# The three written orders of issue of a slot attention and feed-forward kernel, replaced

## The chip, the cores and the metric

The kernel runs on one core of a Trainium2 chip. The time is device microseconds (us) of one launch on that core; lower is better. The median of three runs stands for a kernel, and one further execution is recorded by the hardware profiler. The engines are TensorE (PE: matmuls, with weight loads as PEld), VectorE (DVE), ScalarE (ACT), GpSimd (POOL) and SyncE (SP), which here issues the DMA transfers. Each engine works off its own instructions in program order and waits, at its next instruction, for what that one needs.

## The reference

Attention between 512 positions and 32 slots in both directions, for 8 batches of 8 heads of 64; the reads are joined to 544 rows of 512 per batch. Then a LayerNorm with a gain, a feed-forward layer of 2048 with ReLU, and the residual:

```python
scores = scale * np.matmul(x, state.transpose(0, 1, 3, 2))      # x (8, 8, 512, 64), state (8, 8, 32, 64)
xread = np.matmul(softmax(scores), state)
scores2 = scale * np.matmul(state, x.transpose(0, 1, 3, 2))
sread = np.matmul(softmax(scores2), x)
y = concat([xread, sread], axis=2)                               # to (8, 544, 512)
xn = (y - mu) / np.sqrt(var + 1e-06) * g_ln
out = y + np.maximum(xn @ w_ch1, 0.0) @ w_ch2                    # w_ch1 (512, 2048), w_ch2 (2048, 512)
```

## The kernel before, in words

Every operand of a feed-forward matmul is carried as two 16-bit parts, a high one and a remainder, and a product is the sum of three terms (`TERMS`): high by high and the two mixed ones. The high part is written by ACT and the remainder by DVE.

The 2048 hidden columns are cut into four units u of 512. In each the first product (`first_product`, line 549) is done by seven block products m0 to m6 of twelve matmuls each (line 565). They are of a fast 2 by 2 matrix multiplication: its operands are seven sums of blocks of the normalised rows (the pieces `pc`, which the DMA transposes to `xnT`) and seven of the weight (`w1c`). Their results are put together from the accumulators in `strips`: ACT copies, DVE adds (u2, u3 and their second halves), POOL adds once. ReLU (ACT) and its remainder (DVE) give `hid`. A strip is named here by its unit and what it is: u0 m4 is the fifth product of unit 0. The second product (`second_product`, line 601) multiplies `hid` by `w2h`, twelve matmuls for each unit and each of four row blocks c (line 605), with a DVE add per row block (`xr`) and a store per pair of them.

`attention(b)` (line 251) is one stream of 121 items: loads of x and state (SP), their scale (an absolute maximum, brought across partitions by two small matmuls into `spread`), the 16-bit parts `x` (the program's x16) and `sh`, the transfers that transpose them (`sT`, `xT`, two of the latter), score0 and score1 (line 299), both softmaxes, the transposed weights `ebT`, the read (line 341), the fold (line 354), the exchange of `ea` through DMA (`ek`), the mix into `xr`, and `normalise` (line 406): statistics, the rows `xn`, the pieces, and four transposes to `xnT`. These are called xnT0, xnT2, xnT4 and xnT6 after the first piece in each.

The order of all this is written out by hand. Each function is a generator that yields one item (an instruction or a group of them) after the other, and `issue` takes from several such streams in the order of a string: `a3` is item 3 of the first stream, `b4-6` are items 4 to 6 of the second. Within a stage the order in the string is the program order of every engine's row:

```python
with tc.manual_schedule():
    for item in plan.split() or [...]:
        n = [int(k) for k in item[1:].split("-")]
        drain(streams[ord(item[0]) - ord("a")][n[0]:n[-1] + 1])
```

There are three strings.
- `PLAN` (line 37) is the first stage. Its streams: a is the attention of batch 0, b to e prepare the four units of the first weight (`weights1`, line 482; `raw` in, `w1c` out), f is the first products of batch 0, g to j prepare the second weight (`weights2`, line 516; `w2h`), k is the attention of batch 1, l is the second products of batch 0.
- `BATCH` (line 60) is used six times, for b = 1 to 6: a is the first products of batch b, b its second products, c the attention of batch b + 1.
- `LAST` (line 70): a and b are the products of batch 7, c normalises the 256 state rows of all batches (`state_rows`, line 642, loaded back into `xs`), d and e are their products, half as wide.

Between stages the rows are joined by the tile scheduler: the loads of the next batch stand ahead of some of the last transfers of this one.

Of the kernel before, what the change touches and what calls it, by code (L numbers as in the profile page):

```python
# [34 lines left out]


PLAN = (
# [22 lines left out]
BATCH = (  # L60
# [9 lines left out]
LAST = (  # L70
# [10 lines left out]


class Later:
# [605 lines left out]
```

## Time and profile before

| what | value |
|---|---|
| median of three runs | 857.88 us (855.61 to 859.16) |
| the profiled execution's own time | 858.59 us |
| its span in the trace | 856.5 us |
| mean granted TensorE clock | 0.983 |
| PLAN | 0 to 204.1 us |
| six times BATCH | 204.1 to 730.7 us |
| LAST | 730.7 to 856.5 us |

The first three rows are one launch seen in three ways: the span is what the trace covers, from the first instruction to the last. The stages' bounds are the starts of the first product matmul of the next stage on PE. In rows of the timeline a line holds start, length, engine, source line, operation, what it writes and reads by the program's names, how many instructions were joined, and in brackets the idle time ahead of it with what ended that. Nearly all ACT, DVE, POOL and SP work is recorded by the helper `do` and so has its line, 105; it is told apart by the names of what it writes. In this section's table and in the prediction a batch means a run of BATCH, counted from 1.

### The profile page before, as it was taken

How to read it: one execution, taken by the hardware profiler on the slowest of the kernel's cores; microseconds unless marked ns; L12 is line 12 of the kernel's file. 1: busy time of each engine (PE TensorE's matmuls, PEld its weight loads, DVE VectorE, ACT ScalarE, POOL GpSimd, SP SyncE). 2: the span in 40 equal slices, each digit the busy share in tenths (PEclk: the TensorE clock that was granted, in tenths of full speed). 3: DMA queues.
4: the chain of work that ended last, by engine and by line, in shares of the span. 5: the costliest groups of instructions: out<-in, count | busy, mean ns of one | idle time of the engine just before them, and what ended most of it. 6: DMA issues, size and time to landing. Idle time of an engine off the chain costs nothing.

```text
span 856.5 us, 13363 instructions
## 1 busy us (share of the span) xinstructions
PE 727.6 (85%) x5472; PEld 481.8 (56%) x5472; DVE 550.1 (64%) x894; ACT 373.9 (44%) x624; POOL 143.2 (17%) x101
## 2 busy tenths in 40 slices
PE   0130786699799979998999989998999899999997
PEld 0030554556674667557754865486548654775663
DVE  5899886896784477557755675567556756573330
ACT  4685763554453345136523652365236523342220
POOL 1606001210130112111202120212020202120100
PEclk9999988799999999999999999999999999999999
DMA  9961522336324521362236222623262423302000
GB/s 278 297 180 57 141 98 51 96 96 136 56 46 98 135 57 26 102 131 51 51 79 131 69 56 60 152 56 66 55 149 54 76 53 76 85 2 44 26 25 25
DMA packets 152861, 75.45 MB, mean 88 GB/s; under 512 B 131744, under 2 KB 143520, under 8 KB 152352
## 3 DMA queue, kind: packets, MB, share of 16 engines
q1 hardware_dynamic: 152656, 74.34, 36.1%
q8 instruction: 43, 0.70, 0.4%
q10 hardware_dynamic: 144, 0.26, 0.1%
q14 instruction: 18, 0.15, 0.1%
HBM read 28.57 MB, written 9.44 MB: 44 GB/s over the span
## 4 chain that ended last, share of the span: by engine, by line
PE 69%; DVE 13%; DMA 9%; ACT 3%; issue 3%; SPq 1%; POOL 1%; POOLq 0%; DVEq 0%; ACTq 0%
PE acc L605 38%; PE acc L565 27%; DMA xT<-x 4%; DVE strips L105 2%; DVE w1c L105 2%; DVE hid L105 2%; DVE x L105 2%; ACT raw L105 2%; DVE w_t L105 1%; SPq L105 1%; PE banks L341 1%; PE banks L354 1%; DMA x_f<-in_x_dram 1%; DMA ek<-ek 1%; POOL strips L105 1%
## 5 line engine op out<-in xcount | busy, mean ns | idle before, releaser
L565 PE MATMUL acc<-xnT,w1c 128*128 128x256 f16 (+1 forms) x3024 | 333.1, 270 | 35.5 <-DMA xnT<-pc 23.4
L605 PE MATMUL acc<-w2h,hid 128*128 128x512 f16 x1632 | 360.7, 379 | 0.0
L565 PEld LDWEIGHTS <-w1c 128*128 128x128 f16 x3024 | 284.5, 99 | 85.5 <-issue 43.3
L605 PEld LDWEIGHTS <-hid 128*128 128x128 f16 x1632 | 158.1, 98 | 180.7
L105 ACT ACTIVATE hid<-strips 128x512 f16<-128x512 f32 (+1 forms) x144 | 85.2, 604 | 100.8 <-DVE strips L105 59.4
L105 DVE SCALAR_TENSOR_TENSOR hid<-strips,hid 128x512 f16<-128x512 f32 (+1 forms) x144 | 108.0, 767 | 28.6 <-ACT hid L105 27.8
L105 ACT ACTIVATE strips<-acc,hs 128x512 f32<-128x512 f32 (+1 forms) x96 | 61.7, 659 | 125.9 <-PE acc L565 119.3
L105 DVE SCALAR_TENSOR_TENSOR strips<-acc,hs,strips 128x512 f32<-128x512 f32 (+1 forms) x96 | 68.1, 711 | 67.0 <-PE acc L565 63.8
L105 POOL TENSOR_TENSOR strips<-strips 128x512 f32<-128x512 f32 (+1 forms) x36 | 47.0, 1304 | 381.9 <-DVE strips L105 299.0
L105 DVE BATCH_NORM_STATS2 s<-xr 128x6 f32<-128x512 f32 x32 | 20.7, 685 | 48.5 <-ACT xr L105 48.5
L105 DVE SCALAR_TENSOR_TENSOR xr<-acc,uo,xr 128x512 f32<-128x512 f32 x28 | 20.9, 749 | 34.6 <-PE acc L605 34.6
L105 ACT ACTIVATE xr<-banks,ux 128x1024 f32<-128x1024 f32 x14 | 15.6, 1115 | 60.5 <-PE banks L381 60.5
L105 ACT ACTIVATE pc<-tq 128x512 f16<-128x512 f32 (+1 forms) x27 | 16.3, 605 | 49.1 <-DMA xnT<-pc 33.1
L105 PE MATMUL spread<-idf,w_am 128*2 128x128 f32 x8 | 2.7, 337 | 39.9 <-ACT raw L105 39.9
L105 DVE TENSOR_TENSOR pc<-xn,pc 128x512 f16<-128x512 f32 (+1 forms) x36 | 24.9, 714 | 14.5 <-ACT pc L105 14.5
L105 ACT ACTIVATE xn<-xn,rs 128x512 f32<-128x512 f32 x34 | 22.1, 712 | 25.9 <-POOL rs L105 25.1
L105 POOL TENSOR_TENSOR rs<-rs,mhalf 128x4 f32<-128x4 f32 (+1 forms) x9 | 12.3, 1371 | 126.2 <-DVE rs L105 122.9
L105 DVE TENSOR_TENSOR pc<-tq,pc 128x512 f16<-128x512 f32 (+1 forms) x27 | 24.1, 892 | 10.9 <-ACT pc L105 10.9
L105 DVE SCALAR_TENSOR_TENSOR x<-x_f,x_s,x 128x512 f16<-128x512 f32 x32 | 30.1, 959 | 0.2 <-ACT x L105 0.2
L299 PE MATMUL banks<-xT,sT 128*32 128x512 f16 x128 | 11.1, 435 | 22.4 <-DMA xT<-x 14.9
L105 ACT ACTIVATE pc<-xn 128x512 f16<-128x512 f32 (+1 forms) x36 | 19.9, 597 | 21.0 <-DMA xnT<-pc 21.0
L105 POOL TENSOR_TENSOR ts<-ts,mA 128x1024 f32<-128x1024 f32 x8 | 15.3, 1913 | 68.8 <-DVE mA L105 68.8
(115 smaller groups left out, 631.9 us busy)
## 6 DMA issues: line engine op xcount, KB each, us to landing
raw<-in_moe_w_ch_dram SPq DMA_DIRECT2D x16, 1024.0 KB, 5.8
x_f<-in_x_dram SPq DMA_DIRECT2D x16, 512.0 KB, 5.3
out_dram<-xr SPq DMA_DIRECT2D x16, 512.0 KB, 3.5
ek<-ea SPq DMA_DIRECT2D x56, 64.0 KB, 2.0
ek<-ek SPq DMA_DIRECT2D x7, 512.0 KB, 4.1
s_r<-in_state_dram SPq DMA_DIRECT2D x32, 64.0 KB, 4.5
xnT<-pc SPq DMA_TRANSPOSE x36, 4.3
s_j<-in_state_dram SPq DMA_DIRECT2D x8, 64.0 KB, 5.1
```

The source lines that it names most:

```text
L105: return lambda: f(*map(now, args), **{k: now(v) for k, v in kw.items()})
L299: nc.tensor.matmul(ps[32 * j:32 * j + 32, g], lhsT=sT[:, g, a, 32 * j:32 * j + 32], rhs=xT[:, 4 * g + j].rearrange("p c t -> p (c t)"), st ...
L341: nc.tensor.matmul(ps_z[:, h // 4, :, h % 4], lhsT=x16[:, h * C + c].rearrange("p i d -> p (i d)"), rhs=ebT[:, :, h // 4, c, 32 * (h % 4): ...
L354: nc.tensor.matmul(pr[:, g], lhsT=z4[:, g, i], rhs=fold, start=i == 0, stop=i == 1, skip_group_check=True)
L565: nc.tensor.matmul(ps[:, f * w:(f + 1) * w], lhsT=w1u[:, m, i, k, f * P:(f + 1) * P], rhs=xTk[:, m, j, k], start=begin and f == 0 and k == ...
L605: nc.tensor.matmul(po, lhsT=hid[:, i, q, c * P:(c + 1) * P], rhs=w[:, j, q], start=first and q == 0 and n == 0, stop=last and q == 3 and n ...
```

## The change

Only the three strings differ. Each new string holds the same items as the one it replaces (592, 235 and 258 of them), in another order; streams, loops, tiles and instructions are the same. The new strings take three lines fewer, so line 105 of before is line 102 afterwards, 299 is 296, 565 is 562 and 605 is 602. A line or two of each:

```diff
 PLAN = (
-    "a3 a2 b1 c1 a1 a0 b0 a4-5 c0 a6-13 a27 a60 a17 a28 b6 a18 b7 a22 b8 a24 a14 a25 b9 b20 a23 a19 d1 c7 c6 "
...
+    "c1 a3-4 a0-2 a5-12 c0 b0 a13 a19-20 c7 a14-15 c6 a27 c8 b1 a24-25 a22 a17 c2 a23 c3-4 a18 c9 a28 a60 c5 "
...
 BATCH = (
-    "a23 c0-2 a0 a24 c5 c4 c6 c3 a27 a1 c8 a6 c7 a28 a25 c11 c10 a36 c9 a26 a7 c12-13 a37 a42 a8 c14 a38 a9 "
...
+    "a25 a23-24 a0-1 c1 c9-10 c0 c7 a2 a26 a33 a3 a34 c2 c11 c8 c12 a4-5 a10 c13-14 a6-7 a11 c15 a12 a27 "
...
 LAST = (
-    "a25 c1 c0 a23 a27 a24 c4 a42 a28 a26 c2 a36 c5 c3 c10 a33 a37 a73 c8 a38 a34 a29 a39 a35 a71 a30 c6 a31 "
...
+    "a4-5 c0 c2-3 a23-26 c1 c4-6 c8 a0 c10 a33-34 a2 c7 c9 c15-16 a13 a1 a3 c11-13 a14-15 a6-8 a10-12 a29 a16 "
...
```

In stream a of BATCH items 0 to 22 are unit 0, 23 to 45 unit 1 and so on, so a25 is u1 m1 and a10 is u0 m4. PE's row in a batch began u1 m0, u0 m0 and had 16 products ahead of score1, one between it and score0; now it begins u1 m1, u1 m0, u0 m0, u0 m1, u1 m4 and has 18 products ahead of both, which follow each other. In PLAN the attention of batch 0 and of batch 1 (streams a and k) and the products (f) stand earlier against the weights (b to e, g to j), and the pieces of the normalised rows come in the order 1, 0, 2, 3 instead of 2, 0, 3, 1.

**SP's row, from the transposes at the end of one batch to the softmax of the next, before.** `xnT` are the transposed pieces, `xT` and `sT` the transposed x16 and state, `s_r` a quarter of the state rows, `x_f` and `s_j` the loads of x and state for the batch after.

```order
L105 DMA_TRANSPOSE xnT<-pc 128x16x128 x2
L105 DMA out_dram<-xr 128x1024
L105 DMA_TRANSPOSE xnT<-pc 128x8x128
L105 DMA_TRANSPOSE xnT<-pc 128x16x128
L105 DMA out_dram<-xr 128x1024
L105 DMA_TRANSPOSE xT<-x_3432 128x16x128
L105 DMA_TRANSPOSE sT<-sh 128x4x128
L105 DMA_TRANSPOSE xT<-x_3432 128x16x128
L105 DMA_TRANSPOSE ebT<-eb 128x16x128
```

Now:

```order
L102 DMA_TRANSPOSE xnT<-pc 128x16x128 x2
L102 DMA_TRANSPOSE xnT<-pc 128x8x128
L102 DMA_TRANSPOSE xnT<-pc 128x16x128
L102 DMA out_dram<-xr 128x1024
L102 DMA sread_rows<-sread 64x1x64
L102 DMA out_dram<-xr 128x1024
L102 DMA_TRANSPOSE sT<-sh 128x4x128
L102 DMA s_r<-in_state_dram 32x8x64 x3
L102 DMA_TRANSPOSE xT<-x_3424 128x16x128 x2
L102 DMA s_r<-in_state_dram 32x8x64
L102 DMA_TRANSPOSE ebT<-eb 128x16x128
```

The three loads of `s_r` moved from the end of the batch before to between `sT` and the two `xT`, which now follow each other, and a fourth behind them; `sT` came ahead of both `xT`.

**DVE's row at the end of a batch, before.** `tq` and `pc` are the sums and remainders of the pieces, `xr<-acc` is the add of a row block of the second product.

```order
L105 SCALAR_TENSOR_TENSOR xr<-acc,uo,xr 128x512 x2
L105 TENSOR_TENSOR tq<-xn 128x512
L105 TENSOR_TENSOR pc<-xn,pc 128x512
L105 TENSOR_TENSOR tq<-xn,tq 128x512
L105 TENSOR_TENSOR pc<-tq,pc 128x512
L105 TENSOR_TENSOR pc<-xn,pc 128x512
L105 TENSOR_TENSOR pc<-tq,pc 128x512
L105 SCALAR_TENSOR_TENSOR xr<-acc,uo,xr 128x512
L105 TENSOR_TENSOR pc<-tq,pc 128x512
L105 TENSOR_TENSOR pc<-xn,pc 128x512 x2
L105 SCALAR_TENSOR_TENSOR xr<-acc,uo,xr 128x512
```

Now, the same place (`hid` here are the remainders of unit 3's strips m5, r and u2):

```order
L102 TENSOR_TENSOR tq<-xn 128x512
L102 TENSOR_TENSOR tq<-xn,tq 128x512
L102 TENSOR_TENSOR pc<-xn,pc 128x512
L102 TENSOR_TENSOR pc<-tq,pc 128x512 x2
L102 TENSOR_TENSOR pc<-xn,pc 128x512
L102 SCALAR_TENSOR_TENSOR hid<-strips,hid 128x2x256 x2
L102 TENSOR_TENSOR pc<-tq,pc 128x512
L102 SCALAR_TENSOR_TENSOR hid<-strips,hid 128x2x256
L102 TENSOR_TENSOR pc<-xn,pc 128x512 x2
L102 SCALAR_TENSOR_TENSOR xr<-acc,uo,xr 128x512 x4
```

The adds of the row blocks moved behind all pieces, and the last three remainders of the first product came between the pieces.

**DVE's row where LAST begins, before.** `xs` are the state rows, `strips` ahead of or between their statistics is the add u1 u2 that u1 m4 waits for.

```order
L105 SCALAR_TENSOR_TENSOR xr<-acc,uo,xr 128x512
L105 BN_STATS s_6922<-xs 128x6
L105 SCALAR_TENSOR_TENSOR strips<-acc,hs,strips 128x512
L105 BN_STATS s_6939<-xs 128x6
L105 BN_AGGR mv<-s_6922 128x2
L105 BN_AGGR mv<-s_6939 128x2
```

Now:

```order
L102 SCALAR_TENSOR_TENSOR xr<-acc,uo,xr 128x512 x4
L102 BN_STATS s_6895<-xs 128x6
L102 BN_AGGR mv<-s_6895 128x2
L102 SCALAR_TENSOR_TENSOR strips<-acc,hs,strips 128x512
L102 BN_STATS s_6929<-xs 128x6
L102 BN_AGGR mv<-s_6929 128x2
```

The aggregate of the first pair moved ahead of the add to `strips`; the first statistics stand ahead of it in both.

73 rows, old and new, of tables (BATCH, LAST, PLAN) are left out of this document.

## The prediction

> **What bounds the kernel now.** I read the page first: the span, the busy shares, the 40 slices and the chain that ended last.
>
> ```profile
> span 856.5 us, 13363 instructions
> PE 727.6 (85%) x5472; PEld 481.8 (56%) x5472; DVE 550.1 (64%) x894; ACT 373.9 (44%) x624; POOL 143.2 (17%) x101
> PE   0130786699799979998999989998999899999997
> DVE  5899886896784477557755675567556756573330
> PE 69%; DVE 13%; DMA 9%; ACT 3%; issue 3%; SPq 1%; POOL 1%; POOLq 0%; DVEq 0%; ACTq 0%
> ```
>
> TensorE (PE) bounds everything behind the first five slices; ahead of them VectorE (DVE) is the full one. The same instructions run afterwards, so PE still needs its 727.6 us, and only the 129 us in which it does nothing can change. The windows put that idle time into stages (start:end, length, busy time of PE, PEld, DVE, ACT, POOL, clock, DMA share, GB/s):
>
> ```profile
> 0.00:91.80 91.80, 14.57 (x167) 11.19 (x168) 75.64 (x129) 56.89 (x86) 32.68 (x27) 1.00 0.67 197
> 91.80:204.10 112.30, 94.56 (x631) 61.33 (x631) 93.08 (x158) 59.67 (x95) 14.02 (x9) 0.89 0.40 101
> 204.10:292.50 88.40, 83.39 (x622) 54.97 (x621) 55.67 (x87) 37.54 (x63) 14.07 (x9) 1.00 0.40 83
> 292.50:382.40 89.90, 84.64 (x620) 55.38 (x618) 54.53 (x87) 37.43 (x63) 14.09 (x9) 0.98 0.37 79
> 382.40:469.30 86.90, 83.12 (x621) 54.84 (x620) 55.67 (x87) 37.55 (x63) 14.08 (x9) 1.00 0.38 83
> 642.80:730.70 87.90, 83.19 (x621) 54.81 (x620) 55.47 (x86) 37.55 (x63) 14.08 (x9) 1.00 0.31 66
> 730.70:856.50 125.80, 118.08 (x961) 79.73 (x959) 48.80 (x87) 32.17 (x65) 11.99 (x11) 0.99 0.12 33
> ```
>
> PLAN runs to 204.1, the six runs of BATCH to 730.7, LAST to the end. PE is idle 77.2 us until the first product, 17.7 in the rest of PLAN, 3.7 to 5.3 in each BATCH (the two that are not shown are like the third), 7.7 in LAST.
>
> **BATCH, the largest term (six times).** PE's timeline, from the start of the batch at 382.41, names its waits, and that of DVE and SyncE (SP) the work behind the last of them:
>
> ```profile
> 382.41 8.02 PE L565 MATMUL acc<-xnT,w1c 128*128 128x256 f16 x72
> 400.23 5.40 PE L565 MATMUL acc<-xnT,w1c 128*128 128x256 f16 x48 [1.41 <-DVE strips L105]
> 406.78 0.62 PE L299 MATMUL banks<-xT,sT 128*32 128x512 f16 x8 [1.14 <-DMA sT<-sh]
> 410.03 0.62 PE L299 MATMUL banks<-xT,sT 128*32 128x512 f16 x8 [1.23 <-DMA xT<-x]
> 401.02 0.75 DVE L105 SCALAR_TENSOR_TENSOR x<-x_f,x_s,x 128x512 f16<-128x512 f32 x1
> 401.85 1.33 SPq L105 DMA_TRANSPOSE xT<-x  x1
> 403.28 1.94 SPq L105 DMA_TRANSPOSE sT<-sh  x1
> 405.61 1.85 SPq L105 DMA_TRANSPOSE xT<-x  x1
> xT<-x SPq DMA_TRANSPOSE x2, 4.4
> ```
>
> Three waits, 1.41 + 1.14 + 1.23 = 3.78 us: a product (u0 m4) behind DVE's add; score1 behind sT's landing; score0 behind the second xT (issued 405.61, 4.4 us to landing).
> - The first goes: on DVE the add that u0 m4 needs is now second in the batch, no longer behind seventeen others.
> - SP now issues sT and three s_r loads ahead of both xT. xT1 still waits for the last x16 remainder, at about +19.2 of the batch (now 401.85 - 382.41 = 19.44), but xT0 no longer waits behind sT: about +21.1 (now +23.2). It lands at +25.5 to +26.0.
> - PE now has 18 products ahead of both scores. A product of 12 matmuls takes 8.02 / 6 = 1.34 us, its rows overlapping (1.31 apart); 18 of them and the small matmuls bring PE to score0 at about +24.5. So one wait of 1 to 1.5 us takes the place of three: 3.78 - 1.5 = 2.3, and I count **2.2 us a batch**, 13.2 in six.
> - Batches 1, 2 and 6 take 88.4, 89.9 and 87.9 where the third takes 86.9: 5.5 us together. In batch 2 it is a longer wait for the same xT with slower products behind it:
>
> ```profile
> 321.44 0.82 PE L299 MATMUL banks<-xT,sT 128*32 128x512 f16 x8 [2.72 <-DMA xT<-x]
> 322.19 10.76 PE L565 MATMUL acc<-xnT,w1c 128*128 128x256 f16 x84
> ```
>
> 84 products' matmuls at 8.02 / 72 each would be 9.36, so the 2.72 us wait cost 1.4 more behind it. An earlier xT takes some of this excess away; between 0 and 5.5 I take 2.3. BATCH together: **-15.5**, bounds -20 (every wait gone but 0.5) and -4 (below, where its margins give way).
>
> What costs nothing here: the four s_r loads moved on SP (1.9 us of issue) stand where SP waits for the remainders anyway; if xT were ready sooner, they would cost up to that. ACT's and POOL's rows move with DVE's (37.5 and 14.1 us busy of 87); where one of ACT's evictions falls behind `ea` the margin is about 0.6 us. The softmax items move to where their inputs arrive, under products.
>
> The price is at the batch's end. DVE there does the eight LayerNorm pieces in one block, with two remainders of the last unit (u3) behind four of them, another behind pc6's, and all four output adds last:
>
> ```profile
> 455.81 1.76 DVE L105 TENSOR_TENSOR tq<-xn,tq 128x512 f32<-128x512 f32 x1
> 457.49 0.68 DVE L105 TENSOR_TENSOR pc<-tq,pc 128x512 f16<-128x512 f32 x1
> 464.07 0.69 DVE L105 TENSOR_TENSOR pc<-tq,pc 128x512 f16<-128x512 f32 x1 [1.61 <-ACT pc L105]
> 467.96 1.29 DVE L105 TENSOR_TENSOR pc<-xn,pc 128x512 f16<-128x512 f32 x2 [3.19 <-ACT pc L105]
> 458.85 4.98 SPq L105 DMA_TRANSPOSE xnT<-pc  x2
> 455.43 1.59 POOL L105 TENSOR_TENSOR xn<-xn 128x512 f32<-128x512 f32 x1 [4.34 <-DVE tq L105]
> ```
>
> Summing such durations from the end of mix to u3's remainders gives about 18.9 us, and PE comes to the second product that reads them after 19.2 to 19.4: 0.1 to 0.5 us to spare. A DVE operation beside one of POOL's takes 1.76 instead of 0.68, so one collision more turns that into a wait of 1 us. I take it as kept.
>
> **PLAN.** The first product waits for xnT, and that chain is DVE's own row:
>
> ```profile
> 91.84 5.34 PE L565 MATMUL acc<-xnT,w1c 128*128 128x256 f16 x27 [23.41 <-DMA xnT<-pc]
> 87.30 12.66 SPq L105 DMA_TRANSPOSE xnT<-pc  x4
> 84.32 2.35 DVE L105 TENSOR_TENSOR pc<-xn,pc 128x512 f16<-128x512 f32 x2
> L105 DVE SCALAR_TENSOR_TENSOR w1c<-w_t,w_s,w1c 128x512 f16<-128x512 f32 x11 | 10.7, 1006 | 0.0
> L105 DVE TENSOR_SCALAR raw<-raw 128x1024 uint32<-128x1024 uint32 x12 | 8.6, 721 | 0.0
> 137.08 1.04 PE L299 MATMUL banks<-xT,sT 128*32 128x512 f16 x8 [6.45 <-DMA xT<-x]
> 158.53 1.87 PE L341 MATMUL banks<-ebT,x 128*128 128x64 f16 x32 [6.54 <-DMA ebT<-eb]
> ```
>
> Ahead of the remainder that releases xnT0, DVE has two w1c remainders (1.01 each), three shifts of raw (0.72), two other pieces (half of 2.35 and one of 0.68 above, 1.9) and sread fewer: 2.0 + 2.2 + 1.9 + about 1.5 of small ones = 7.6. So xnT0 would be issued near 79.7 instead of 87.30, and the first product would start near 84.2. That is no gain yet. The weight work moved behind it is still due, PE waits for it (the w2 scale's broadcast near 93, u2's weights near 100) and then, at score0 of the second batch's attention, now early in PE's row, for xT near 116. Past that, attention(1) stands far earlier on DVE: the remainder of eb after 121 us of DVE work, not 135, so the 6.54 us wait for ebT goes, and the 6.45 us wait for xT turns into the one near 116. By hand I find PE about 4 us ahead at 138 and PLAN's end at 195 to 197.5, so **-6.5**. Bounds: 0, when all is handed back at the waits named, and -12, when the first product's lead is kept (7.6) with most of the ebT wait.
>
> **LAST.**
>
> ```profile
> 739.28 18.50 PE L565 MATMUL acc<-xnT,w1c 128*128 128x256 f16 x168 [1.87 <-DVE strips L105]
> 737.88 0.70 DVE L105 BATCH_NORM_STATS2 s<-xs 128x6 f32<-128x512 f32 x1 [6.23 <-DMA xs<-sread_rows]
> 739.74 0.30 DVE L105 BATCH_NORM_AGGREGATE mv<-s 128x2 f32<-128x6 f32 x2
> 758.87 3.33 PE L565 MATMUL acc<-xnT,w1c 128*128 128x256 f16 x29 [1.08 <-ACT strips L105]
> ```
>
> DVE's row still begins with the state rows' statistics, which wait for a load, ahead of the add that u1 m4 needs. PE now reaches u1 m4 one product earlier and the add has the aggregate ahead of it too: 1.87 + 1.31 + about 0.2 = 3.4 us, 1.5 more; the 1.08 us wait may go. Bounds -1 and +1.5, I take **+0.5**. The tail (one add, four stores) is the same instructions in the same order.
>
> **Sum.** 858.59 (the profiled execution; its span is 856.5, and it lies 0.7 above the median of 857.88) - 15.5 - 6.5 + 0.5 = **837.1**.
>
> **Rivals.**
> - *PLAN gives nothing.* The earlier first product is handed back at score0's wait near 116 and later at w2's weights. For it: DVE is 83% busy in PLAN's second part. Against: 13 us in two waits for attention(1) stand there now. 858.6 - 15.5 + 0.5 = 843.6.
> - *BATCH's margins give way.* A second product waits 1 to 2 us for u3's remainders in each batch: 6 x 1.5 = 9 back, and PLAN as forecast: 846.
> - *More of both* (PLAN -10, BATCH -18): 831.
> - *The clock pays.* The single wait for xT0 becomes 2.7 us, as at 321.44, and each batch then pays 1.2 more in the wait and 1.4 behind it: 6 x 2.6 = 15.6, so 852.7. Against: waits of 1.1 to 1.4 us in the third batch cost no clock (1.00). The Trainium skill's page "TensorE: Matmul & The Clock Gate", section "Part 1: The HAM clock gate (the "warmup" mystery)", has the clock halved only after an idle window of about 3.4 us; by that, no wait foreseen in BATCH would cost clock and this rival is void. The row with 10.76 does not agree: there 2.72 us was enough.
> - *Slower than before.* DVE stops in its row at the remainder of pc6, which waits for ACT's pc6 and this for xnT2's landing; behind it stand a remainder of u3, two more pieces and all four output adds. Now pc6 starts 464.07 - 458.85 = 5.2 us after the first xnT issue, and I find 2.5 us to spare. It decides past 7.7 us; each us beyond costs six. To eat the 21.5 gained and 4.3 more it takes 25.8 / 6 = 4.3 us beyond, a landing 12 after the issue, and gives 863. Against: the row at 467.96, behind the pair's second transfer, came 9.1 after the first issue, and no transfer here was slower.
>
> **How the numbers follow.** Chances: forecast (831 to 844) 0.44; PLAN nothing 0.17; margins 0.17; more of both 0.08; clock 0.07; slower 0.07. What a measurement of this kernel tells from no change is about 0.5%, 4.3 us, so faster means under 854. Faster: 0.44 + 0.17 + 0.08, 0.14 of the margins' case (it may take two places in a batch) and 0.02 of the clock's = 0.85; same: 0.03 + 0.05 = 0.08; slower 0.07. The range takes in -20 and -12 in part, 826, and the clock's case, 853; outside are the slower case and some 0.1 of the tails.
>
> **What would show it.** Right: the first product near 84; BATCH windows of 84 to 85 us with one wait ahead of score0 and none at u0 m4 or score1; PLAN ending at 195 to 198; u1 m4 in LAST waiting 3 us or more. Wrong: a wait of PE for `hid` or `xr` late in the batches (margins), products past 0.12 us a matmul behind score0 (clock), PLAN's end near 204, or a DVE idle stretch ahead of pc6 with the adds behind it.

## The result, and the profile after

The changed kernel takes 826.97 us (median of 4 runs, 825.11 to 827.74), before it was 857.95 (4 runs, the three above and one more): the ratio is 0.9639, with a 95% interval of 0.9613 to 0.9665. The profiled execution took 826.83 us, its span is 825.0. The page of the profile after, its first lines and the chain that ended last:

```profile
span 825.0 us, 13446 instructions
PE 725.5 (88%) x5472; PEld 481.6 (58%) x5472; DVE 540.8 (66%) x894; ACT 366.2 (44%) x624; POOL 151.4 (18%) x101
PE   0140868899999999998999999999999999899997
DVE  4999879795767476746774676567656765662221
PE 73%; DVE 14%; DMA 7%; issue 3%; ACT 3%; SPq 0%; DVEq 0%; ACTq 0%
```

PE's busy time is the same within 2.1 us (727.6 before); the idle time went from 129 to 99.5 us. By stages (windows of the changed kernel, columns as before):

```profile
0.00:83.20 83.20, 15.32 (x167) 11.54 (x168) 70.85 (x120) 52.68 (x80) 35.89 (x27) 1.00 0.72 207
83.20:193.40 110.20, 94.55 (x631) 59.91 (x631) 94.27 (x166) 63.00 (x101) 15.87 (x10) 0.92 0.47 115
193.40:277.70 84.30, 82.74 (x620) 54.99 (x619) 54.73 (x87) 36.49 (x63) 14.59 (x9) 1.00 0.40 85
362.10:446.90 84.80, 82.58 (x620) 54.91 (x619) 54.76 (x87) 36.50 (x63) 14.57 (x9) 1.00 0.41 92
446.90:530.60 83.70, 82.69 (x621) 54.98 (x620) 54.76 (x87) 36.48 (x63) 14.57 (x9) 1.00 0.38 85
698.20:825.00 126.80, 119.33 (x961) 80.41 (x959) 47.28 (x87) 31.54 (x65) 12.21 (x11) 0.99 0.10 29
```

From these bounds, read off the first product matmul of each stage:

| stage | before | after | difference | forecast |
|---|---|---|---|---|
| to the first product | 91.84 | 83.23 | -8.6 | -7.6 |
| all of PLAN | 204.15 | 193.41 | -10.7 | -6.5 |
| six times BATCH | 526.55 | 504.80 | -21.75 | -15.5 |
| LAST, to PE's end | 121.04 | 122.05 | +1.0 | +0.5 |
| behind PE's end | 4.8 | 4.7 | 0 | 0 |

The fourth batch shows what the prediction spoke of. PE's timeline from its start, and SP's:

```profile
446.95 9.33 PE L562 MATMUL acc<-xnT,w1c 128*128 128x256 f16 x84
457.95 13.27 PE L562 MATMUL acc<-xnT,w1c 128*128 128x256 f16 x120
471.15 0.61 PE L296 MATMUL banks<-xT,sT 128*32 128x512 f16 x8
472.78 0.61 PE L296 MATMUL banks<-xT,sT 128*32 128x512 f16 x8 [1.01 <-DMA xT<-x]
460.19 1.22 SPq L102 DMA_TRANSPOSE sT<-sh  x1
461.46 1.56 SPq L102 DMA_DIRECT2D s_r<-in_state_dram  x3
465.87 4.46 SPq L102 DMA_TRANSPOSE xT<-x  x2
```

One wait of 1.01 us, ahead of score0, where three of together 3.7 us stood; the 18 products and score1 run without a break up to it. (In the second batch score1 waits too: 0.72 us, and then score0 1.00.) xT is issued at 465.87 - 446.95 = +18.9 of the batch. At the batch's end DVE and PE stand as close as foreseen:

```profile
518.72 1.28 DVE L102 SCALAR_TENSOR_TENSOR hid<-strips,hid 128x512 f16<-128x512 f32 x2
521.74 0.69 DVE L102 TENSOR_TENSOR pc<-tq,pc 128x512 f16<-128x512 f32 x1 [1.74 <-ACT pc L102]
519.79 10.96 PE L602 MATMUL acc<-w2h,hid 128*128 128x512 f16 x50
```

The two remainders of u3 (strips m5 and r) are done at 520.00; the second product that reads r's begins at 520.22 in the middle of PE's unbroken run, which ends at 530.58 with four products of 2.59 us. That is 0.2 us to spare, counted to the start of the product. In the program its third matmul is the first that reads a remainder (the third of `TERMS`), and in run 7 the wait stands there (46 of the four products' 48 matmuls come behind it), so the margin was up to 0.4 us wider.

### The profile page after: what moved, and what is told of

It is laid out like the page before. It is cut to its first block, busy times and chain, and to the rows that moved or that the text cites. A ratio compares the mean times of both kernels' runs of the same rounds, so it can differ in the third digit from the quotient of the medians.

```text
span 825.0 us, 13446 instructions
## 1 busy us (share of the span) xinstructions
PE 725.5 (88%) x5472; PEld 481.6 (58%) x5472; DVE 540.8 (66%) x894; ACT 366.2 (44%) x624; POOL 151.4 (18%) x101
## 4 chain that ended last, share of the span: by engine, by line
PE 73%; DVE 14%; DMA 7%; issue 3%; ACT 3%; SPq 0%; DVEq 0%; ACTq 0%
PE acc L602 41%; PE acc L562 28%; DMA xT<-x 4%; DVE x L102 2%; DVE w1c L102 2%; DVE strips L102 2%; DVE w_t L102 1%; DMA x_f<-in_x_dram 1%; DVE hid L102 1%; PE banks L378 1%; PE banks L338 1%; DVE raw L102 1%; ACT raw L102 1%; PE banks L351 1%; PE banks L296 1%
## 5 line engine op out<-in xcount | busy, mean ns | idle before, releaser
L102 ACT ACTIVATE hid<-strips 128x512 f16<-128x512 f32 (+1 forms) x144 | 80.5, 597 | 78.5 <-DVE strips L102 43.3
L102 DVE SCALAR_TENSOR_TENSOR hid<-strips,hid 128x512 f16<-128x512 f32 (+1 forms) x144 | 92.1, 663 | 16.4 <-ACT hid L102 16.2
L102 DVE TENSOR_TENSOR pc<-xn,pc 128x512 f16<-128x512 f32 (+1 forms) x36 | 35.9, 1013 | 10.8 <-ACT pc L102 10.7
L102 POOL TENSOR_TENSOR ts<-ts,mA 128x1024 f32<-128x1024 f32 x8 | 17.2, 2149 | 92.7 <-DVE mA L102 90.0
L102 DVE SCALAR_TENSOR_TENSOR strips<-acc,hn,strips 128x512 f32<-128x512 f32 (+1 forms) x32 | 22.8, 711 | 16.1 <-PE acc L562 15.2
L102 ACT ACTIVATE pc<-xn 128x512 f16<-128x512 f32 (+1 forms) x36 | 20.8, 595 | 17.9 <-DMA xnT<-pc 17.8
L102 DVE TENSOR_TENSOR pc<-tq,pc 128x512 f16<-128x512 f32 (+1 forms) x27 | 18.2, 691 | 11.6 <-ACT pc L102 11.6
L102 ACT ACTIVATE ea<-ef 128x1024 f16<-128x1024 f32 x8 | 8.4, 1055 | 38.0 <-DVE ef L102 38.0
```

Of the source, the lines that this page charges most:

```text
L102: return lambda: f(*map(now, args), **{k: now(v) for k, v in kw.items()})
```

## The experiments

Ratios are to the kernel before, run on the same chip. The changed kernel itself stands at 0.9639.

**1 to 3: each string alone.** Before's program with one of the three new strings.

```diff
-PLAN = (before)      BATCH = (before)      LAST = (before)
+PLAN = (after)       # e1, the others as before
+BATCH = (after)      # e2
+LAST = (after)       # e3
```

> Before with the new PLAN alone. If the three stages add up, the whole of PLAN's share of the difference shows: the first batch's first product at 193.4 instead of 204.2, so -10.7 us (847). If PLAN's lead is used up later (the first batch waits for loads or transposes that are not earlier), between 0 and -5. The forecast had -6.5 for this stage.

> Before with the new BATCH alone. If the stages add up: six batches in 504.8 instead of 526.6 us, -21.8 us (836). If part of the gain belongs to the state that PLAN leaves behind, less: the forecast's own terms give -13 to -15.5 (843).

> Before with the new LAST alone: u1 m4's wait grows from 1.87 to 2.7 us and more, +1.0 us (859) if the stages add up. A rival, that this loss comes only from the new batch's late last add ahead of the load of xs, would give -0.5 to 0.

Measured: PLAN alone 846.1 us, ratio 0.9870 (0.9852 to 0.9888); BATCH alone 835.28, 0.9746 (0.9730 to 0.9761); LAST alone 859.26, 1.0015 (0.9999 to 1.0031). As parts of 858 us that is -11.2, -21.8 and +1.3, together -31.7, and the whole change measured -31. In the traces PLAN ends at 193.56 in the first, the six batches take 505.5 in the second, and LAST 122.9 in the third. The stages add up. In the third the added time alone is within its measurement's uncertainty; its trace shows it (122.9 against 121.0), with a wait of 3.35 us ahead of u1 m4.

**4: the first of the three waits of a batch, alone.** In the kernel before one add moves ahead on DVE.

```diff
-... a2 a5 c32 c34 c30 a40 c35 c26 c33 a19 a3 c24 ...
+... a2 a5 c32 c34 a3 c30 a40 c35 c26 c33 a19 c24 ...
```

> Before with one item of BATCH moved: the add that u0 m4 waits for (u0 u2) stands ahead of two x16 remainders on DVE. Its wait of 1.42 us goes in both theories. If the three waits of a batch are worth their sum, -1.42 x 6 = -8.5 us. If they are one chain that ends at the second xT's landing, PE reaches score1 and score0 earlier, waits there 1.4 us longer, and the time does not move (0 to -1).

Measured: 857.8 us, ratio 1.0016 (0.9998 to 1.0033). PE's timeline of the third batch:

```profile
393.36 6.84 PE L564 MATMUL acc<-xnT,w1c 128*128 128x256 f16 x61
408.00 1.01 PE L298 MATMUL banks<-xT,sT 128*32 128x512 f16 x8 [2.67 <-DMA sT<-sh]
408.94 2.71 PE L564 MATMUL acc<-xnT,w1c 128*128 128x256 f16 x12
411.59 0.61 PE L298 MATMUL banks<-xT,sT 128*32 128x512 f16 x8
```

The wait ahead of u0 m4 is gone and score1's has grown from 1.14 to 2.67. The three waits were one chain, and what ends them is the landing of sT and xT. Of the 2.2 us a batch that the prediction summed, none comes from the add alone. (Behind the longer wait twelve matmuls take 2.71 us, not 1.47; more on that below.)

**5: sT between the two xT again.** The changed kernel, one item moved on SP.

```diff
-... c22 c23 a13 a14 ... c33 c20 a47 c37 ...
+... c22 a13 a14 ... c33 c23 c20 a47 c37 ...
```

> The changed kernel with one item of BATCH moved on SP alone: sT stands between the two xT again. The second xT is then issued 1.7 us later and lands near +27.0 of the batch, so the one wait ahead of score0 grows from 1.0 to about 2.2 us: +1.2 x 6 = +7 us. If a wait of that length also costs clock (the rival of the forecast), 1.4 more in each batch: +15. If the position of sT does not matter, 0.

Measured: 840.23 us, ratio 0.9791 (0.9769 to 0.9813), 13.3 above the changed kernel. PE's timeline of the third, fourth and fifth batch:

```profile
393.12 0.61 PE L296 MATMUL banks<-xT,sT 128*32 128x512 f16 x8 [3.86 <-DMA xT<-x]
393.67 5.77 PE L562 MATMUL acc<-xnT,w1c 128*128 128x256 f16 x36
...
479.78 1.04 PE L296 MATMUL banks<-xT,sT 128*32 128x512 f16 x8 [2.37 <-DMA xT<-x]
480.76 5.23 PE L562 MATMUL acc<-xnT,w1c 128*128 128x256 f16 x36
...
566.28 0.61 PE L296 MATMUL banks<-xT,sT 128*32 128x512 f16 x8 [2.33 <-DMA xT<-x]
566.83 4.10 PE L562 MATMUL acc<-xnT,w1c 128*128 128x256 f16 x36
```

The waits ahead of the scores add up to 16.0 us in the six batches against 8.5 in the changed kernel: +7.5, as the first theory has it. The batches together take 12.6 longer (517.4 against 504.8), and the 5 us that are left are products at a lower clock in three of them (granted 0.98 in the first, third and fourth, 1.00 in the others): behind the waits of 3.86 and 2.37 us the same 36 matmuls took 5.77 and 5.23 us, behind 2.33 they took 4.10. So both theories were half right: a wait of such a length may cost some 1.6 us more, or nothing.

**6: more products ahead of the scores.** The changed kernel with u3 m1 (a71) ahead of them.

```diff
-... a47 c37 c76 a37 c28 a49 a51 c36 ... c49 a71 a52 ...
+... a47 a71 c37 c76 a37 c28 a49 a51 c36 ... c49 a52 ...
```

> The changed kernel with one more product (u3 m1) ahead of the two scores. If that wait is only a matter of how many products stand ahead, 1.0 us a batch goes, -6 to -7 us in all. If the softmax chain behind it has no room left (ebT's landing has 1.6 us ahead of the read, the exchange of ea 0.9 ahead of mix), part of it comes back as waits there: -2 to -4. If there is no room at all, 0.

Measured: 828.58 us, ratio 0.9647 (0.9630 to 0.9665): no gain. PE's timeline at the second and fifth batch:

```profile
320.58 1.09 PE L338 MATMUL banks<-ebT,x 128*128 128x64 f16 x32 [1.18 <-DMA ebT<-eb]
...
586.04 0.79 PE L378 MATMUL banks<-sk,ek 128*128 128x64 f16 x16 [1.55 <-DVE strips L102]
```

The waits ahead of score0 are gone in four batches and smaller in two (0.42 and 1.07); new ones stand ahead of the read (0.61, 1.18) and of mix (0.44, 1.55, 1.37). In the fifth batch of the changed kernel the last exchange of `ek` is issued at 580.54 and lands 4.1 us later, at about 584.65, and mix starts at 584.75: score0 to mix is a chain about as long as PE's work beside it. In this run that exchange is issued at 581.50 and takes up to 4.5 us; the wait of 1.55 ends with it, though the row names `strips`, which DVE had finished at 585.36. A later start comes back as a wait further on: the six batches take 504.8 us in both.

**7: one remainder behind pc6.** The changed kernel; b3, the second product that reads it, follows it in the string.

```diff
-... a87 c112 a78 b3 c118 c119 a85 ...
+... a87 c112 c118 c119 a78 b3 a85 ...
```

> The changed kernel with one remainder of unit 3 (r) on DVE moved two places, behind the remainder of pc6, which waits for xnT2's landing. If DVE's order at the batch's end is the tight place that the forecast named (0.2 us to spare now), the second product that reads it waits until about 523.1 where it starts at 520.2 in the fourth batch: 2.9 x 6 = +17 us, and a wait of that length in each batch may cost clock besides (+25). If DVE has room there, 0.

Measured: 849.36 us, ratio 0.9885 (0.9858 to 0.9912), 22.4 above the changed kernel. DVE's and PE's timeline in the fourth batch of this run:

```profile
534.69 0.69 DVE L102 TENSOR_TENSOR pc<-tq,pc 128x512 f16<-128x512 f32 x1 [2.34 <-ACT pc L102]
535.30 1.28 DVE L102 SCALAR_TENSOR_TENSOR hid<-strips,hid 128x512 f16<-128x512 f32 x2
536.04 4.28 PE L602 MATMUL acc<-w2h,hid 128*128 128x512 f16 x19 [2.27 <-DVE hid L102]
```

DVE stands still for 2.34 us at pc6 and PE with it; five batches show such a wait (2.24 to 2.33), the sixth one of 0.58, and PE's busy time rises by 6.9 us, to 732.4, through slower matmuls. This is the margins' rival, and the slower case in small: two places in DVE's row cost 19.6 us in the six batches (524.4 against 504.8); PLAN, 2.1 longer, is within its scatter, and LAST took 1.7 more.

**8 and 9: LAST's first wait.** In 8 only the add (a26) goes ahead of the first statistics; in 9 the state rows' first eleven items go behind the first products' copies and adds.

```diff
-a4-5 c0 c2-3 a23-26 c1 c4-6 c8 a0 c10 a33-34 a2 c7 c9 c15-16 a13 a1 a3 c11 ...
+a4-5 c0 a23-26 c2-3 c1 c4-6 c8 a0 c10 a33-34 a2 c7 c9 c15-16 a13 a1 a3 c11 ...      # e8
+a4-5 c0 a23-26 c1 a0 a33-34 a2 a13 a1 c2-3 a3 c4-6 c8 c10 c7 c9 c15-16 c11 ...      # e9
```

> The changed kernel with one add of LAST (u1 u2) ahead of the first statistics of the state rows on DVE. The wait of 2.73 us ahead of u1 m4 goes: -2.5 to -2.9 us. If another wait stands right behind it (an accumulator that is not free, or a later strip on DVE behind the statistics that wait for xs), -0.5 to -1.5.

> The changed kernel with the first eleven items of the state rows in LAST (statistics, xn, the first pieces) moved, on DVE, ACT and POOL alike, behind the first products' own copies and the add u1 u3. The load of xs then holds up nothing that PE waits for early: 2.7 us less, 824.3. If the add u0 u2 or a later strip still stands behind the statistics, about half of it, 825.6; if the wait only moves again, as when the add alone was moved, 0.

Measured: 828.13 us (ratio 0.9648, 0.9633 to 0.9663) and 826.14 us (0.9623, 0.9599 to 0.9646). The first is a miss. Its PE and ACT timelines:

```profile
712.26 3.00 PE L562 MATMUL acc<-xnT,w1c 128*128 128x256 f16 x26 [2.63 <-ACT strips L102]
710.46 0.72 ACT L102 ACTIVATE xn<-xn,rs 128x512 f32<-128x512 f32 x1 [6.66 <-POOL rs L102]
711.54 0.67 ACT L102 ACTIVATE strips<-acc,hs 128x512 f32<-128x512 f32 x1
```

The wait moved three products on: on ACT, too, a copy that PE needs stands behind work on the state rows. With all of them moved (9), LAST takes 118.0 us to PE's end instead of 122.05, 4.05 less, with no wait left. That is more than the wait's 2.73: behind it, in the changed kernel, products also ran slowly. Its DVE row shows the load that all of this waits for:

```profile
704.73 0.69 DVE L102 BATCH_NORM_STATS2 s<-xs 128x6 f32<-128x512 f32 x1 [5.57 <-DMA xs<-sread_rows]
698.21 5.40 PE L562 MATMUL acc<-xnT,w1c 128*128 128x256 f16 x48
706.34 5.92 PE L562 MATMUL acc<-xnT,w1c 128*128 128x256 f16 x40 [2.73 <-DVE strips L102]
```

By the second row 40 matmuls take 4.5 us; they took 5.92. Over the whole kernel the two medians, taken on different chips, differ by 0.8 us, which doesn't separate 9 from the changed kernel; its trace shows the gain in LAST and longer other stages (PLAN 0.9, the third batch 1.5). The latter is clock, at the same order: the third batch of the changed kernel, and that of run 9.

```profile
389.15 0.62 PE L296 MATMUL banks<-xT,sT 128*32 128x512 f16 x8 [2.22 <-DMA xT<-x]
389.70 4.10 PE L562 MATMUL acc<-xnT,w1c 128*128 128x256 f16 x36
...
390.20 1.04 PE L296 MATMUL banks<-xT,sT 128*32 128x512 f16 x8 [2.10 <-DMA xT<-x]
391.17 5.27 PE L562 MATMUL acc<-xnT,w1c 128*128 128x256 f16 x36
```

Runs 7, 8 and 11, in which the order around the scores is the same, show it as run 9 does (waits of 2.21, 2.32 and 2.35; the 36 matmuls took 5.25, 5.09 and 5.13). The profiled execution of the changed kernel was the lucky one of five.

**10: two products fewer ahead of the scores.**

```diff
-... a36 a18 a46 a8 a48 a9 c33 c20 a47 c37 c76 a37 c28 a49 a51 c36 c39 a38 c40 c4 c34-35 c38 c49 a71 ...
+... a36 a18 a8-9 c20 c76 a37 c33 c37 c28 c36 c39-40 c4 c34-35 c38 c49 a46 a48 a47 a49 a51 a38 a71 ...
```

> The changed kernel with two products (u2 m0, u2 m1) behind the scores instead of ahead of them in PE's row of BATCH, DVE's maximum and transpose for the softmax ahead of the add that reads them. If the time of a batch is the landing of the second xT plus PE's work behind score0, the wait there grows by 2 x 1.31 and so does each batch: 1.31 x 2 x 6 = +15.7 us, and up to 1.5 a batch more where the longer wait costs clock (+25). If a batch is set by the chain from score0 to mix instead, those products fill room behind score0 and the time stays within 3 us.

Measured: 853.2 us, ratio 0.9937 (0.9914 to 0.9960), 26.2 above the changed kernel: the upper figure. The waits ahead of the scores add up to 23.5 us, 15.1 more than in the changed kernel (2 x 1.31 x 6 = 15.7 was expected); the other 11 is clock (PE's busy time is 736.0, 10.5 more). The third batch:

```profile
396.45 0.62 PE L296 MATMUL banks<-xT,sT 128*32 128x512 f16 x8 [1.79 <-DMA xT<-x]
398.82 0.61 PE L296 MATMUL banks<-xT,sT 128*32 128x512 f16 x8 [1.76 <-DMA xT<-x]
399.37 8.39 PE L562 MATMUL acc<-xnT,w1c 128*128 128x256 f16 x60
```

In this run's sixth batch, behind waits of 1.67 and 1.87 us, 60 such matmuls took 6.72 us. With the changed kernel both ways round (6 and 10), its place of the scores is a good one: one product later gains nothing, two earlier lose 26 of the 31 us; one earlier was not measured.

**11: the first product's lead given back.** In PLAN six DVE operations on weights return to where they delay xnT0, with four ACT items that feed them.

```diff
-... b19 a93 a91 d20 e22 a94 f2 f0 e30 e24-25 g2 d17 h7 d21-22 e31 e23 a95 ... h4 ... g3 ...
+... b19 e22 e30 e24-25 e31 e23 h7 h4 g2-3 a93 a91 d20 a94 f2 f0 d17 d21-22 a95 ...
```

> The changed kernel with six DVE operations on weights (three w1c remainders, two shifts, one 'or', 4.8 us by their durations) put back ahead of the pieces that release xnT0 in PLAN. The first product then starts near 88 instead of 83.2. If the lead of the first product is kept to the end of PLAN, +4.8 us (832). If it is handed back at score0's wait for xT near 106 to 113, as the forecast argued, 0 to +1 (827 to 828), and the gain of PLAN is then the earlier attention of the second batch.

Measured: 830.66 us, ratio 0.9688 (0.9662 to 0.9713), 3.7 above the changed kernel. PE's timeline:

```profile
87.25 5.69 PE L562 MATMUL acc<-xnT,w1c 128*128 128x256 f16 x36 [19.85 <-DMA xnT<-pc]
118.12 1.04 PE L296 MATMUL banks<-xT,sT 128*32 128x512 f16 x8 [6.78 <-DMA xT<-x]
```

In the changed kernel the same rows are at 83.23 [15.38] and 112.90 [6.80]. The wait ahead of score0 doesn't shrink when the first product comes later; the transfer it waits for comes later too. PLAN ends at 198.72, where the eight traces with the changed kernel's PLAN end at 192.5 to 195.5. So the lead is kept to the end of PLAN, other than the forecast argued.

**12: the x16 remainders sooner, with 9's LAST.** On DVE alone, in BATCH and PLAN. In the program either xT waits for the last of the four remainders, not for its own two: xT is taken from the pair of buffers that held x_f, which all four read.

```diff
 BATCH
-... a13 a14 c5 c26 c31-32 a19 c29-30 c27 a28 c24 a20 a35 a40 c25 ...
+... a13 c5 c26-27 a14 c31-32 a19 c29-30 a28 c24-25 a20 a35 a40 ...
 PLAN
-... k34-35 a57 f15-16 d34 g17 k29 k23 f21 k32 k28 k36 k30 k33 ...
+... k34 k32 a57 f15 d34 k29-30 k35 f16 g17 k23 f21 k28 k36 k33 ...
```

> The changed kernel with the state rows of LAST later (as in the ninth run), and on DVE alone the x16 remainders earlier: in BATCH the second one ahead of the add u0 u2b and the first one ahead of u0 u3b, in PLAN the last two ahead of sklo and of a remainder of unit 0. Both xT are written where x_f lies and so wait for all four remainders. If score0's wait is that of DVE's row, xT is issued 1.35 us sooner in a batch and the wait of 1.0 goes together with the whole chain behind it: -1.0 x 6 and what the longer waits of batches 1 to 3 shrink by, -7 in BATCH, -2 in PLAN and -4 in LAST: 814. If the chain from score0 to mix has no room, as when the scores alone were moved later, the waits move to read and mix: only LAST's and PLAN's part, 821 to 823.

Measured: 816.03 us (5 runs, 813.71 to 816.37), ratio 0.9506 (0.9486 to 0.9527), faster than both kernels. The fourth batch, PE and SP, and two windows:

```profile
459.78 7.70 PE L562 MATMUL acc<-xnT,w1c 128*128 128x256 f16 x69
467.40 1.31 PE L296 MATMUL banks<-xT,sT 128*32 128x512 f16 x16
461.12 4.45 SPq L102 DMA_TRANSPOSE xT<-x  x2
360.40:443.20 82.80, 82.58 (x620) 54.90 (x619) 54.93 (x87) 36.51 (x63) 14.23 (x9) 1.00 0.39 93
443.20:525.90 82.70, 82.62 (x620) 54.91 (x619) 54.80 (x87) 36.52 (x63) 14.22 (x9) 1.00 0.38 86
```

xT is issued at 461.12 - 443.21 = +17.9 of the batch, 1.0 sooner, both scores run through, and in these two windows (the third and fourth batch) 0.1 to 0.2 us is left idle. The second batch keeps a wait of 1.07. The six batches take 497.9 us (-6.9, as expected), LAST 118.0 (-4.06, as expected). PLAN's part is a miss: score0 there comes 2.15 us earlier, at 110.75, and PLAN ends at 193.58, where the changed kernel's ends at 193.41. Of the lead, 1.5 us are left at PE's last wait in PLAN, which ends at 163.37 where it ended at 164.87; behind it 24 matmuls took 4.45 us where they took 2.78 (granted clock from there to the end 0.94 and 1.00), and that used it up in this trace.

## Why the prediction was right, and where it was mis-sized

- **The time**: 826.97 us is 10 below the forecast of 837.1, under its band (831 to 844) and less than 1 us inside the low bound of 826. It is nearer to the rival *More of both* (831, a chance of 0.08) than to the forecast: the terms of BATCH and PLAN were too small by 6.25 and 4.2, both on the same side.
- **What bounds it, and which waits can go**: right. PE's work stayed, idle time went, and the stages add up (runs 1 to 3).
- **BATCH, the mechanism**: right. The first product's wait, score1's and part of score0's were replaced by one, which hangs on xT. Runs 5 and 10 give the two parts a price: sT ahead of both xT, and 18 products ahead of both scores. Each is worth more than half of the stage's gain if it is taken away alone, since the clock goes with the wait; run 4 shows that the third part, the add, is worth nothing alone.
- **BATCH, the size**: -21.75 where -15.5 was forecast. Two terms were too small. "1 to 1.5 us takes the place of three" was counted as 1.5 and measured 1.0 (3.73 to 0.99 in the batches compared here); and each wait that goes takes some 0.15 us of drained matmuls along: 72 of them took 8.02 us and 12 took 1.47, so 0.109 each and 0.16 for a run's end. A batch without excess went from 86.8 us (the third to fifth before) to 83.75 (the fourth to sixth after): 3.05, not 2.2. And of the 5.8 us by which batches 1, 2 and 6 were longer (the prediction read 5.5), all but 1.3 went, where 2.3 was taken; the third batch has a new excess of 1.1 (its wait is 2.22). Sum: 6 x 3.05 + 4.5 - 1.1 = 21.7.
- **PLAN**: the first product at 83.23, forecast near 84.2: that count of DVE's row was right. The step that failed is the next one, "That is no gain yet", by which the lead is handed back at PE's later waits. The wait for xT ended at 112.90, not near 116, and run 11 shows why it isn't a fixed date: with the first product 4.0 us later it came 5.2 later. DVE's row ahead of those remainders has adds that read the first products, so it moves with them (in run 11 DVE stands still for 2.51 us for a product at the add at 107.12). In this pair of traces PLAN gained 10.7 and the first product 8.6. Single traces scatter: in the four with the old PLAN the first product starts at 90.1 to 91.8 and PLAN ends at 203.7 to 205.1, in the eight with the new one at 82.9 to 83.3 and 192.5 to 195.5; the means differ by 7.9 and 10.2. What gives the 2 us on top of the lead was not tested; the wait for ebT, 6.54 us before, is gone.
- **LAST**: right in place, and in sign by the clock. The wait ahead of u1 m4 is 2.73, not 3.4 (behind the old BATCH, in run 3, it is 3.35), and the 1.08 went as forecast, so the two waits together shrank from 2.95 to 2.73; slow products behind the one that is left took another 1.4, which the sum didn't hold. +1.0 in all, forecast +0.5, inside its bounds.
- **The margins' rival**: 0.2 us were to spare at u3's remainders, as worked out (0.1 to 0.5, counted to the start of the product), and they held in every batch. Run 7 shows what their failing would have cost.
- **The clock's rival**: it did not come in the size that was forecast (six waits of 2.7 us), since five of six waits ahead of score0 are at most 1.56. But it is not void: the third batch's wait of 2.22 us cost nothing in this execution (36 matmuls in 4.10 us) and some 1.5 us in the four others named under run 9, and LAST's cost 1.4 here.
- **The slower case**: xnT2's landing left 2.4 us to spare in the fourth batch (the remainder behind pc6's is done at 523.04, the product that reads it begins at 525.40), forecast 2.5.

## What to carry to other kernels

Waits that follow each other on the bounding engine may be one chain: ask what the last of them hangs on before adding them up, and test by removing the first (run 4). A gain at the start of a stage is not lost at a later wait if what that wait hangs on is queued behind work fed by the start (run 11). And read from the program's waits what really releases a transfer: here it was the last of four remainders, and moving two of them up by one place in DVE's row brought 7 us more in BATCH.

## What the runs showed of the hardware

How much clock a wait costs is not a matter of its length alone. Waits of 2.22, 2.33 and 2.54 us had products at full speed behind them (36 matmuls in 4.10 us); one of 2.10 had 5.27, one of 2.37 had 5.23, one of 2.73 had 1.4 us more, and two of 1.79 and 1.76 with one product's work between them had 8.39 instead of 6.72 for 60, where two of 1.67 and 1.87 had 6.72. Where a single wait ahead of score0 cost anything (seven times in runs 5, 7, 8, 9 and 11), the price hardly depended on its length either: 1.4 to 1.6 us behind 2.10 to 2.58, 1.7 behind 3.86, taking the score's own matmuls and the products behind it together. The Trainium skill, page "TensorE: Matmul & The Clock Gate", section "Part 1: The HAM clock gate (the "warmup" mystery)", describes a window of about 3.4 us that runs free of the kernel's start, and half clock after an idle one. That the same length costs once and once not agrees with a window that runs free; that waits well under 3.4 us cost at all does not agree with a window that has to be idle throughout. These runs don't tell how the gate counts. Why the xT transfer of one early batch lands later than that of the others (a wait of 2.22 in the third here, 2.72 in the second before) was not settled either. It isn't issued later: both xT go at +18.9 in the third batch as in the fourth, but the second of them takes 6.0 us to land instead of 4.9; in the second batch before it is 5.9 where the third has 4.4.
